# A decode step of two cached-attention layers: buffer base moved to a 256-byte boundary, and one long load per row and layer split unevenly over the DMA engines

## The chip, the core and the metric

The kernel runs on one core of one Trainium2 chip. A core has five engines that matter here: TensorE (PE in the profile; its weight loads are listed apart as PEld), VectorE (DVE), ScalarE (ACT), GpSimd (POOL) and SyncE (SP), which in this kernel issues every DMA. Transfers between the chip's main memory (HBM) and the on-chip buffer of 128 partitions (SBUF) are carried out by the core's 16 DMA engines. The metric is the device time of one execution in microseconds (us).

## The reference, cut to what matters

One token per sequence, eight sequences (B = 8), width D = 640, 32 heads of width 128, and a cache of 4096 keys and values per head. The block is applied twice, with the same caches and weights:

```python
def _A_ref(x, k_cache, v_cache, wq, wo):        # attention over the cache
    q = (x @ wq) as [B, 32, 1, 128]
    scores = einsum("bhqd,bhkd->bhqk", q, k_cache) * 128 ** -0.5
    o = einsum("bhqk,bhkd->bhqd", softmax(scores), v_cache)
    return o as [B, 1, 4096] @ wo
def _B_ref(x, w1, w2):                          # dense layer, 640 -> 1728 -> 640
    return relu(x @ w1) @ w2
x = A_x
x = x + _A_ref(layernorm(x), k_cache, v_cache, wq, wo)
x = x + _B_ref(layernorm(x), w1, w2)
x = x + _A_ref(layernorm(x), k_cache, v_cache, wq, wo)
x = x + _B_ref(layernorm(x), w1, w2)
```

Keys and values of one sequence are 32 x 4096 x 128 values each, 64 MiB for both in bfloat16. Both layers need them, so the two layers together read nearly 1 GB if little is kept between them; every byte is used for one multiplication per layer.

## The kernel before

The host lays keys (transposed) and values of a sequence side by side in one array `A_kv` of shape [8, 128, 131072]: for each sequence and each of the 128 partitions one contiguous row of 256 KiB, in the order in which the kernel reads it. The smallest piece that the kernel handles is a **unit**: 128 partitions x 2048 values (4 KiB per partition, 512 KB in all), a quarter of the keys or of the values of a pair of heads.

**The arena.** `arena` (L346) is one SBUF tile of G = 26 units. Loads put units of `A_kv` into it, PE uses each unit once per visit, and a unit's place is then free for another load. Keys are used at L575 (each 128 x 128 block is loaded as PE's weights, the query is the moving column), values at L563 (the softmax weights `P_sb` are PE's weights, the values move). For a sequence, the units that layer 0 read last stay in the arena (`keep`, 21 of them) for layer 1, and two more are parked in PSUM (`stash`), so that layer 1 begins with data that is already there.

**The order.** `plan` (L34) writes the whole program as one list of operations before anything is issued: pairs of heads (visits) of layer 0 of the next sequence alternate in blocks with those of layer 1 of the present one, and the tail of each layer (output projection, dense layer, norms) is put between matmuls as small steps. The list is executed in this order on every engine (a manual schedule: nothing is reordered). The planner keeps a rough clock of PE and of the loads; from the lead of the loads over PE it chooses how many units one load takes (`LEADS`, L22: 8, 4 or 2 units, otherwise 1), within `feed` (L109), which is called whenever a unit's place is freed and appends `("load", b, p, n, u)`: sequence, place in `A_kv`, number of units, place in the arena. A "long" load is one of 8 units: 128 rows of 32 KiB, 4 MB.

In the list there are 536 loads: 235 of one unit, 41 of two, 17 of three, 100 of four, 16 of five and 127 of eight. While the kept units hold most of the arena, around the change from layer 0 to layer 1 of each sequence, 27 to 29 loads of one unit follow each other; this happens eight times. Between these stretches of single units lie nine stretches with long loads, each with six to seventeen of them.

**The loads.** `do_load` (L527) issues one DMA on SP's queue for each load:

```python
def do_load(b, p, n, u):
    nc.sync.dma_start(out=arena[:, u * GW : (u + n) * GW], in_=A_kv[b, :, p * GW : (p + n) * GW])
```

Before it issues, SP waits until PE has finished with the units that are overwritten, and until the DMA eight before it has landed, since the completion semaphores are eight, taken in turn. PE in turn waits for the landing of a load before its first use of a unit of it.

**Where things lie.** Tiles lie in SBUF in the order of their pools: `consts` first, then the weights (`w1_sb`, `w2_sb`, `wq_sb`, `wo_sb`), then `arena`, then the small tiles (`sm`). The tile `wo_sum` (L339), 16 bytes per partition, is in `consts`; it holds row sums of `wo` that are computed once on DVE in `do_ws` (L407) and read by PE in `do_w` (L640). With it the weights and the arena start 32 bytes past a multiple of 256: the arena's first byte is at 119,072 of its partition.

Of the kernel before, what the change touches and what calls it, by code (L numbers as in the profile page):

```python
# [10 lines left out]
BF16 = mybir.dt.bfloat16  # L11
# [10 lines left out]
LEADS = ((9, 8), (6, 4), (5, 2))  # L22
SOON = 4
AHEAD = 2
BANK = 512
CAP = 20


# [5 lines left out]
def plan(B, NP, n_up, n_down):  # L34
# [35 lines left out]
    for which, i in slots:  # L70
        layer, b, hp = visits[i]
# [14 lines left out]
    lands = [0.0] * G  # L86
    where, kept, ready = {}, {}, {}
    ops, chains = [], []
    at = [0, 0]
    clock = [5.0, 6.0]  # L90

    def keeps(which, i, g):
# [7 lines left out]
    def place(x):  # L100

        return visits[x[1]][1], tile_at(NP, x[0], visits[x[1]][2]) * UNIT + x[2], keeps(*x)

    def room(n):

        us = [u for u in range(G - n + 1) if not any(owner[u : u + n])]
        return min(us, key=lambda u: max(freed[u : u + n])) if us else None

    def feed():  # L109

        while at[0] < len(stream):
            most = next((n for least, n in LEADS if clock[1] - clock[0] >= least), 1)
            most = min(most, max(1, (len(stream) - at[0]) // 2), max(1, (G - len(kept) - 2) // 3))
            b, p, keeping = place(stream[at[0]])
            n = 1
            while n < most and place(stream[at[0] + n]) == (b, p + n, keeping):
                n += 1
            u = room(n)
            if u is None:
                return  # L120
            for k, (which, i, g) in enumerate(stream[at[0] : at[0] + n]):
                ops.extend(("weights",) + w for w in weights.pop(i, []) if which == "K")
                owner[u + k] = True
                where[which, i, g] = u + k
                if keeping:
                    kept[which, b, visits[i][2], g] = u + k
            at[0] += n
            clock[1] = max(clock[1], clock[0] + 1.4) + 0.1 + 1.2 * n
            lands[u : u + n] = [clock[1] + 2] * n
            ops.append(("load", b, p, n, u))  # L130

    def find(which, i, g):
        u = where.get((which, i, g))
        return kept[which, visits[i][1], visits[i][2], g] if u is None else u

    def release(which, i, g):
        key = which, visits[i][1], visits[i][2], g
        u = where.pop((which, i, g), None)
        at[1] += 1
        if key in kept:  # L140
            if visits[i][0] == 0:
                return
            u = kept.pop(key)
        if visits[i][0] == 0 and stashed(which, i, g) is not None:
            ops.append(("stash", stashed(which, i, g), u))
        owner[u], freed[u] = False, at[1]
        x = uses[at[1] + SOON] if at[1] + SOON < len(uses) else None
        if x and visits[x[1]][0] and stashed(*x) is not None:
            u = where[x] = room(1)
            owner[u] = True  # L150
            lands[u] = clock[0] + 2
            ops.append(("unstash", stashed(*x), u))
        feed()
# [10 lines left out]
    def step():  # L164

        n = 0
        for c in sorted(chains, key=lambda c: c[0][0]):
            if not n or n + c[0][0] <= CAP:
                n += c[0][0]
# [13 lines left out]
    def finish(layer, b):  # L183
# [13 lines left out]
        return c  # L197

    feed()
    for which, i in slots:  # L200
        layer, b, hp = visits[i]
# [10 lines left out]
        for g in range(UNIT):  # L212
            u = find(which, i, g)
# [39 lines left out]
def kernel(  # L253
# [12 lines left out]
    nc = tc.nc  # L266
    P = nc.NUM_PARTITIONS
# [11 lines left out]
    GW = W // UNIT  # L279
# [10 lines left out]
    consts = ctx.enter_context(tc.tile_pool(name="consts", bufs=1))  # L290
    wres = ctx.enter_context(tc.tile_pool(name="wres", bufs=1))
    kv = ctx.enter_context(tc.tile_pool(name="kv", bufs=1))
    sm = ctx.enter_context(tc.tile_pool(name="sm", bufs=2))
# [13 lines left out]
    def load_weights(which, g=0):  # L307
# [15 lines left out]
        out=ident, in_=ident, pattern=[[-1, P]], compare_op=ALU.not_equal,  # L323
# [12 lines left out]
    for c in range(4):  # L336
        rows = slice(32 * c, 32 * c + CJ)
        nc.vector.tensor_copy(out=gsel[rows, :, c // 2], in_=ident[rows, rows])
    wo_sum = consts.tile([P, 2, 2, 2], BF16, name="wo_sum")  # L339
    eps_c = consts.tile([P, 1], FP32, name="eps_c")  # L340
    nc.vector.memset(eps_c, eps)
    xT = consts.tile([P, B, DC], FP32, name="xT")
# [1 line left out]
    q0 = consts.tile([P, H, B], BF16, name="q0")  # L344
    o1 = consts.tile([P, H, B], BF16, name="o1")
    arena = kv.tile([P, G * GW], BF16, name="arena")  # L346
    OR = 96 + CJ
    o_ps = ps.tile([P, CJ * Dh], FP32, name="o_ps")
    s_ps = ps.tile([P, 2, 2 * NJ], FP32, name="s_ps")
    blk_ps = ps.tile([P, BANK], FP32, name="blk_ps")  # L350
    oy_ps = ps.tile([P, BANK], FP32, name="oy_ps")
    stash_ps = [ps.tile([P, 2 * BANK], BF16, name=f"stash{n}_ps") for n in range(STASH * GW // (2 * BANK))]
    per = len(stash_ps) // STASH
    nc.vector.memset(o_ps, 0.0)

    up_parts = [range(f, min(f + 3, FC)) for f in range(0, FC, 3)]
    visits, ops = plan(B, NP, len(up_parts), DC)
    q1, s_tiles, P_tiles, m_tiles, o_tiles, blk, oy, invL, oT, nmax, st = ({} for _ in range(11))

# [154 lines left out]
    def do_stash(slot, u):  # L514
        for n, t in enumerate(stash_ps[slot * per : (slot + 1) * per]):
            nc.vector.tensor_scalar(
                out=t.bitcast(mybir.dt.int32),
                in0=arena[:, u * GW + n * 2 * BANK : u * GW + (n + 1) * 2 * BANK].bitcast(mybir.dt.int32),
                scalar1=0, scalar2=None, op0=ALU.bitwise_or,
            )  # L520

    def do_unstash(slot, u):
        for n, t in enumerate(stash_ps[slot * per : (slot + 1) * per]):
            copy = nc.vector.tensor_copy if n % 2 else nc.scalar.copy
            copy(out=arena[:, u * GW + n * 2 * BANK : u * GW + (n + 1) * 2 * BANK], in_=t)

    def do_load(b, p, n, u):  # L527
        nc.sync.dma_start(out=arena[:, u * GW : (u + n) * GW], in_=A_kv[b, :, p * GW : (p + n) * GW])

    def do_q0(g):  # L530

# [89 lines left out]
    def do_oc(i):  # L621
        o_tiles[i] = sm.tile([P, CJ, Dh], BF16, name="o_sb", bufs=1)
        nc.scalar.copy(out=o_tiles[i][:OR], in_=o_ps[:OR, :].rearrange("p (j d) -> p j d", j=CJ))  # L623

    def do_og(i):
        oy[i] = oy_ps[:, : 2 + DC * B]
        for j in range(CJ):
            nc.tensor.matmul(  # L628
                oy[i][:, :2], lhsT=o_tiles[i][:OR, j, :], rhs=gsel[:OR, j, :], start=(j == 0), stop=(j == CJ - 1)
            )  # L630
# [27 lines left out]
    def do_y(i):  # L658
# [3 lines left out]
        nc.vector.tensor_tensor(out=xT[:, b0 : b0 + nb, :], in0=xT[:, b0 : b0 + nb, :], in1=y, op=ALU.add)  # L662

    does = dict(WS=do_ws, S=do_s, YC=do_yc, load=do_load, stash=do_stash, unstash=do_unstash, weights=load_weights, mm=do_mm, M1=do_m1, T=do_t, M2=do_m2, B=do_b, E=do_e,
                L=do_l, I=do_i, OC=do_oc, OG=do_og, O=do_o, W=do_w, Y=do_y, C=do_finish, Q0=do_q0, Q=do_q, QC=take_q)

# [65 lines left out]
```

## Time and profile before

| | |
|---|---|
| median of 3 runs | 2388.94 us (2388.45 to 2391.3) |
| the profiled execution | 2390.05 us |
| its span, first to last instruction | 2388.2 us |
| granted TensorE clock | 1.0 |
| PE busy | 1281.9 us (54%) |
| PE weight loads busy | 792.0 us (33%) |
| DVE, ACT busy | 383.6 us (16%), 386.2 us (16%) |
| moved by DMA | 996.01 MB, mean 417 GB/s over the span |
| PE idle before L563, before L575 | 628.2 us, 313.7 us, nearly all ended by a load's landing |

Times and counts are of one profiled execution. Where the page gives a wait, it names the instruction that waited, what ended the wait, the total in us, how often, and the longest. A DMA of a tile is named by the tiles: `arena<-in_A_kv_dram` is a load of `do_load`. "SPq" is SP's queue of DMA issues. The chain that ended last is found by going back from the last instruction, at each step to what released it.

### The profile page before, as it was taken

To read this page: it belongs to the slowest core of one execution; us is meant where nothing else is said; L and a number is where in the kernel's file an instruction comes from. 1 tells how busy PE (TensorE), PEld (TensorE's weight loads), DVE (VectorE), ACT (ScalarE), POOL (GpSimd) and SP (SyncE) were. 2 spreads that over 40 slices of the span, in tenths; PEclk is the share of its full clock that TensorE was granted. 3 is DMA by queue.
4 is the path that set the end of the run, shared out by engine and by line. 5 is a ranking of instruction groups with operands and counts; after the bars stand their busy time and mean duration, and the time that the engine had idled before them with its cause. 6 is when DMAs were issued, how large, how long until landed. Compare 5 with 4: busy or idle time off the path is not lost.

```text
span 2388.2 us, 57845 instructions
## 1 busy us (share of the span) xinstructions
PE 1281.9 (54%) x26522; PEld 792.0 (33%) x26522; DVE 383.6 (16%) x1889; ACT 386.2 (16%) x1177; POOL 39.3 (2%) x190
## 2 busy tenths in 40 slices
PE   3437544574544844558444574446644466544845
PEld 2325322252323522225222352224422244222523
DVE  1103111121111211112111221112111121111211
ACT  1112111121111211112111121111211112111211
POOL 0000000000000000000000000000000000000000
DMA  9999999999999999999999999999999999999997
GB/s 409 426 426 392 429 427 430 426 385 430 429 429 424 397 428 427 433 420 398 431 427 430 405 412 428 427 431 403 416 428 428 427 398 414 427 430 426 392 429 308
DMA packets 78968, 996.01 MB, mean 417 GB/s; under 512 B 8836, under 2 KB 8836, under 8 KB 38916
## 3 DMA queue, kind: packets, MB, share of 16 engines
q1 hardware_dynamic: 78724, 992.32, 98.9%
q8 instruction: 207, 3.39, 0.6%
q14 instruction: 37, 0.30, 0.0%
HBM read 992.27 MB, written 0.01 MB: 415 GB/s over the span
## 4 chain that ended last, share of the span: by engine, by line
DMA 77%; PE 16%; ACT 3%; DVE 2%; issue 1%; POOL 0%; SPq 0%; POOLq 0%; DVEq 0%; ACTq 0%
DMA arena<-in_A_kv_dram 77%; PE s_ps L575 7%; PE o_ps L563 4%; ACT P_sb L604 2%; DVE hmx L589 1%; PE blk_ps L547 1%; PE oy_ps L628 1%; ACT nmax L600 1%; PE blk_ps L594 1%; PE oy_ps L450 1%; PE oy_ps L645 1%; PE blk_ps L585 1%; PE blk_ps L609 1%; DVE diag L591 0%; ACT o_sb L623 0%
## 5 line engine op out<-in xcount | busy, mean ns | idle before, releaser
L563 PE MATMUL o_ps<-arena,P_sb 128*4 128x512 bf16 x4096 | 559.4, 603 | 628.2 <-DMA arena<-in_A_kv_dram 625.9
L575 PEld LDWEIGHTS <-arena 128*128 128x128 bf16 x16384 | 495.2, 104 | 443.8 <-DMA arena<-in_A_kv_dram 418.2
L575 PE MATMUL s_ps<-q_97,arena 128*128 128x1 bf16 x8192 | 272.9, 166 | 313.7 <-DMA arena<-in_A_kv_dram 308.1
L563 PEld LDWEIGHTS <-P_sb 128*4 128x4 bf16 x4096 | 95.7, 82 | 710.7 <-issue 692.2
L600 ACT ACTIVATE nmax<-blk_ps 128x2 f32<-128x2 f32 x128 | 22.0, 172 | 1051.5 <-PE blk_ps L594 1051.5
L589 DVE TENSOR_REDUCE hmx<-blk_ps 2x1 f32<-2x128 f32 x256 | 71.3, 279 | 606.2 <-PE blk_ps L585 605.4
L623 ACT CAST o_sb<-o_ps 100x512 bf16<-100x512 f32 x256 | 149.8, 585 | 112.4 <-PE o_ps L563 109.5
L600 ACT ACTIVATE nmax<-blk_ps,q_scale 128x2 f32<-128x2 f32 x128 | 33.6, 262 | 652.7 <-PE blk_ps L594 650.5
L615 DVE TENSOR_REDUCE lsum<-blk_ps 128x2 f32<-128x64 f32 x256 | 57.4, 224 | 450.9 <-PE blk_ps L609 450.8
L581 DVE TENSOR_REDUCE mrow<-s_ps 128x2 bf16<-128x64 f32 x256 | 57.6, 225 | 334.7 <-PE s_ps L575 299.4
L609 PEld LDWEIGHTS <-onesb_c 128*128 128x128 bf16 x256 | 26.7, 104 | 200.7 <-issue 200.7
L604 ACT ACTIVATE P_sb<-s_ps,nmax,q_scale 128x32 bf16<-128x32 f32 x256 | 82.6, 373 | 4.3
L585 PE MATMUL blk_ps<-ident,mrow 128*2 128x128 bf16 x256 | 73.7, 288 | 0.0
L638 DVE TENSOR_TENSOR oT<-oy_ps,invL 128x2 bf16<-128x2 f32 x128 | 20.4, 159 | 320.6 <-PE oy_ps L628 320.6
L628 PE MATMUL oy_ps<-gsel,o_sb 100*128 100x2 bf16 x1024 | 66.1, 168 | 8.0 <-DVE xc L493 1.8
L594 PEld LDWEIGHTS <-onesb_c 2*128 2x128 bf16 x256 | 25.2, 98 | 125.2 <-issue 124.9
L609 PE MATMUL blk_ps<-P_sb,onesb_c 128*128 128x64 bf16 x256 | 57.2, 224 | 8.9 <-ACT P_sb L604 0.2
L604 ACT ACTIVATE P_sb<-s_ps,nmax 128x32 bf16<-128x32 f32 x256 | 59.4, 283 | 4.1
L628 PEld LDWEIGHTS <-o_sb 100*128 100x128 bf16 x1024 | 49.5, 108 | 23.5 <-ACT o_sb L623 10.0
L594 PE MATMUL blk_ps<-diag,onesb_c 2*128 2x2 bf16 x256 | 41.7, 163 | 25.8 <-DVE diag L591 0.4
L575 PE MATMUL s_ps<-q_30433,arena 128*128 128x1 bf16 x1024 | 34.5, 166 | 38.3 <-DMA arena<-in_A_kv_dram 37.4
L547 PE MATMUL blk_ps<-xq,wq_sb 128*128 128x1 bf16 x1280 | 52.2, 165 | 3.0 <-DVE hmx L589 2.6
(191 smaller groups left out, 822.3 us busy)
## 6 DMA issues: line engine op xcount, KB each, us to landing
arena<-in_A_kv_dram SPq DMA_DIRECT2D x127, 4096.0 KB, 25.1
arena<-in_A_kv_dram SPq DMA_DIRECT2D x100, 2048.0 KB, 24.3
arena<-in_A_kv_dram SPq DMA_DIRECT2D x235, 512.0 KB, 6.8
arena<-in_A_kv_dram SPq DMA_DIRECT2D x41, 1024.0 KB, 11.8
arena<-in_A_kv_dram SPq DMA_DIRECT2D x16, 2560.0 KB, 22.9
arena<-in_A_kv_dram SPq DMA_DIRECT2D x17, 1536.0 KB, 24.8
wq_sb<-in_A_wq_dram SPq DMA_DIRECT2D x4, 1280.0 KB, 30.2
wo_sb<-in_A_wo_dram SPq DMA_DIRECT2D x4, 1280.0 KB, 30.0
```

The lines of the kernel that those rows point to most:

```text
L547: nc.tensor.matmul(q_ps[:, h : h + 1], lhsT=wq_sb[:, g, c, (2 * n + h) * Dh : (2 * n + h + 1) * Dh], rhs=xlns[b][:, 0, c : c + 1], start=( ...
L563: nc.tensor.matmul(o_ps[32 * c : 32 * c + CJ, :], lhsT=P_tiles[i][:, h, j : j + CJ], rhs=arena[:, at + c * CJ * Dh : at + (c + 1) * CJ * D ...
L575: nc.tensor.matmul(s_tiles[i][:, j : j + 1], lhsT=arena[:, at + n * P : at + (n + 1) * P], rhs=q, start=True, stop=True)
L581: nc.vector.tensor_reduce(out=m_tiles[i], in_=s_tiles[i].rearrange("p (h j) -> p h j", h=2), axis=AX.X, op=ALU.max)
L585: nc.tensor.matmul(blk[i][:2, :P], lhsT=m_tiles.pop(i), rhs=ident, start=True, stop=True)
L589: nc.vector.tensor_reduce(out=hmx, in_=blk[i][:2, :P], axis=AX.X, op=ALU.max)
L594: nc.tensor.matmul(blk[i][:, P : P + 2], lhsT=ones_b, rhs=nmax.pop(i), start=True, stop=True)
L600: nc.scalar.activation(out=nm, in_=blk[i][:, P : P + 2], func=ACT.Copy, scale=less)
L604: nc.scalar.activation(out=P_tiles[i][:, h, :], in_=S[:, h, :], func=ACT.Exp, bias=nm[:, h : h + 1], scale=more)
L609: nc.tensor.matmul(blk[i][:, P + 2 :], lhsT=ones_p, rhs=P_tiles[i].rearrange("p h j -> p (h j)"), start=True, stop=True)
L623: nc.scalar.copy(out=o_tiles[i][:OR], in_=o_ps[:OR, :].rearrange("p (j d) -> p j d", j=CJ))
L628: nc.tensor.matmul(oy[i][:, :2], lhsT=o_tiles[i][:OR, j, :], rhs=gsel[:OR, j, :], start=(j == 0), stop=(j == CJ - 1))
```

## The change

Two edits.

The first moves the small tile `wo_sum` from the pool `consts` to the pool `sm`, which lies after the arena. All tiles between, the weights and the arena, move 32 bytes down: the arena starts at 119,040, a multiple of 256.

The second counts the loads of 8 units. The planner starts counting anew at each load of one unit, and marks a load of 8 units as "tilted" when it is the fifth since then. `do_load` issues a tilted load in three DMAs instead of one: partitions 0 to 111, then 112 to 119, then 120 to 127, with the same columns. Nine of the 127 long loads are marked, one in each of the nine stretches. The rest of the list of operations is the same.

```diff
@@ -23,6 +23,7 @@
 SOON = 4
 AHEAD = 2
 BANK = 512
+TILTED = (5,)
 CAP = 20
@@ plan
-    at = [0, 0]
+    at, long = [0, 0], [0]
@@ feed
             lands[u : u + n] = [clock[1] + 2] * n
-            ops.append(("load", b, p, n, u))
+            long[0] = 0 if n == 1 else long[0] + (n == LEADS[0][1])
+            ops.append(("load", b, p, n, u, n == LEADS[0][1] and long[0] in TILTED))
@@ the kernel's tiles
-    wo_sum = consts.tile([P, 2, 2, 2], BF16, name="wo_sum")
     eps_c = consts.tile([P, 1], FP32, name="eps_c")
...
     arena = kv.tile([P, G * GW], BF16, name="arena")
+    wo_sum = sm.tile([P, 2, 2, 2], BF16, name="wo_sum", bufs=1)
@@ do_load
-    def do_load(b, p, n, u):
-        nc.sync.dma_start(out=arena[:, u * GW : (u + n) * GW], in_=A_kv[b, :, p * GW : (p + n) * GW])
+    def do_load(b, p, n, u, tilted):
+
+        for rows in (slice(0, 112), slice(112, 120), slice(120, P)) if tilted else (slice(0, P),):
+            nc.sync.dma_start(out=arena[rows, u * GW : (u + n) * GW], in_=A_kv[b, rows, p * GW : (p + n) * GW])
```

## The prediction

> **What bounds the kernel now.** I read the slices first, then the chain, then two stretches set side by side.
>
> ```profile
> span 2388.2 us, 57845 instructions
> ...
> DMA  9999999999999999999999999999999999999997
> GB/s 409 426 426 392 429 427 430 426 385 430 429 429 424 397 428 427 433 420 398 431 427 430 405 412 428 427 431 403 416 428 428 427 398 414 427 430 426 392 429 308
> ...
> q1 hardware_dynamic: 78724, 992.32, 98.9%
> q8 instruction: 207, 3.39, 0.6%
> ...
> DMA 77%; PE 16%; ACT 3%; DVE 2%; issue 1%; POOL 0%; SPq 0%; POOLq 0%; DVEq 0%; ACTq 0%
> ```
>
> The DMA engines are busy in every slice, at 425 to 433 GB/s except in a dip about every five slices, and 77% of the chain that ended last is loads into `arena`. Beside the loads runs a small stream, q8: 207 instruction fetches. The dips are the stretches of single-unit loads, once per batch row:
>
> ```profile
> core 0: us, PE busy (x) PEld busy (x) DVE busy (x) ACT busy (x) POOL busy (x), PEclk, DMA share, GB/s
> 590.00:760.00 170.00, 79.47 (x1627) 47.41 (x1627) 22.76 (x115) 23.28 (x74) 0.00 (x0) 1.00 1.00 428
> 784.00:822.00 38.00, 32.73 (x724) 24.38 (x725) 9.49 (x51) 9.13 (x28) 4.82 (x23) 1.00 0.99 385
> ```
>
> In the long stretch PE is busy 47% of the time and the DMA engines set the pace; in the 38 us stretch PE is busy 86% and loads wait for it to free units. The chain of waits around the border of the two:
>
> ```profile
> 744.07 20.27 DMA arena<-in_A_kv_dram
> 764.41 21.03 DMA arena<-in_A_kv_dram
> 785.49 0.58 PE s_ps L575 x16
> ```
>
> So up to 785.49 us the chain is one load after another, and from there it is PE's. What ended the last DMA step is the completion of the load issued at 764.4. The trace's DMA records (start, duration and bytes of each packet, completion times; no engine's number) give that load's sixteen completions: 0, 0.5, 0.7, 1.1, 1.3, 1.5, 1.7, 1.8 us after the first, then 4.4, 4.8, 4.9, 5.0, 5.2, 5.3, 5.6, 5.8. The last of them is at 785.45 us, and PE starts there. **Eight engines run some 4 us behind the other eight, and PE waits for the slowest.** At the next dependent load the fast ones stand idle: first completions step by 4.3 us there, where a unit takes 1.28, while the last engine steps by 1.27 and never rests. The same jump ends each row's long stretch; the spread of completions just before it is 4.1, 5.9, 5.8, 5.5, 5.9, 5.8, 5.7 and 4.8 us, and 3.8 at the program's end.
>
> Why eight: packets on one engine follow each other within 3 to 4 ns, so they can be strung into sixteen chains. Each q8 fetch (16,384 bytes) breaks one chain for about 1.05 us and lengthens a packet beside it by about 0.5, and the chain that fetch n hits is the one that fetch n+8 hits (seen in three stretches of 160 to 180 us). So eight fixed engines carry all fetches, about three each per row.
>
> [...]the 40-row load of `x_bf` has ten completions. [...]the nearest case here is `w1`, whose odd rows begin 128 bytes off in HBM: some take 651 ns where the line through 16,384 bytes (614 ns) and 17,920 (671 ns) gives 647. [...]
>
> **The change, part by part.**
>
> 1. *Tilt.* The plan's list of operations stays as it is; nine of its 536 loads, each of 4 MB, become three DMAs. They are the fifth long load of each long stretch, so one comes before each of the eight borders and one before the end. A row of the load is 32,768 bytes and takes 1.216 us. Engines of the first half get nine rows instead of eight, those of the second seven: +1.216 and -1.216 us each time. If the eight that fetch are the second half, the last completion before each border comes 1.216 us sooner. It cannot be overtaken by the fast half: their latest stand at 1.1 to 2.7 us on the scale above, so after the tilt at 2.3 to 3.9, and the slow half's latest at 2.9 to 4.7. Only at the end is it close (1.4 + 1.2 against 3.8 - 1.2), and 1.20 is kept. From a border on the chain is PE's, so all that follows starts sooner by as much, and after each border the two groups are mixed again, so the gain is made anew: 8 x 1.216 + 1.20 = **10.9 us**.
> 2. *Its price.* Eighteen DMAs more on SP, about 0.45 us of SP each by the first issues (0.7, 1.2, 1.6, 2.1 us): 8 us in all. Behind them on SP stand the next loads. SP issues a long load 20 to 25 us before it lands, with a load or two still queued in front. Its longest wait, in us, times and the longest one, is for earlier loads:
>
> ```profile
> SPq L528 <- DMA arena<-in_A_kv_dram: 1139.9, 307, 13.5
> ```
>
> and the page's list of issues gives the time to landing:
>
> ```profile
> arena<-in_A_kv_dram SPq DMA_DIRECT2D x127, 4096.0 KB, 25.1
> ...
> arena<-in_A_kv_dram SPq DMA_DIRECT2D x235, 512.0 KB, 6.8
> ```
>
>    That cover hides it: 0. Without it, 0.9 us per tilt would be exposed. Completion semaphores go round eight lanes, so each tilt moves later DMAs two lanes on; a long stretch has three or four loads in flight, five or six with a tilt, so no lane is waited for. PE's first matmuls on the eight units wait for three lanes in place of one; PE idles half of that stretch: 0, at most 0.1 us times nine.
> 3. *Alignment.* `wo_sum` (16 bytes, in a 32-byte place) leaves the pool ahead of the weights, and `arena` moves from 119,072 bytes, 32 past a multiple of 256, to 119,040, a multiple. No instruction changes. No row with an aligned destination is in the trace, so I bound it: at least 0 (no packet or byte is added, which excludes a loss; writes may not care), at most the 3.7 ns per row of `w1`. I take 1.18 ns, the time of 32 bytes at the slope of the packet times. On the path lie the rows outside the single-unit stretches: (536 - 235 single loads + 10 weight loads) x 8 rows per engine = 2488, so 0 to 9.2 us, taken **2.9**. The other 1880 rows lie in stretches that PE sets: 0 taken, at most 7.
>
> Sum: 10.9 + 2.9 = 13.8 us. The profiled execution took 2390.05 us around its span of 2388.2, 1.1 above the median of 2388.94. So 2376.2 there and **2375.1** against the median.
>
> **Rivals.** A measurement of this kernel can tell about 0.2% (4.8 us) from no change.
>
> - *A, as summed:* 2375, from 2362 (alignment at its upper bounds, 16 us) to 2380 (alignment nothing, a little lost). For it: nine borders of one pattern, and a shift between the halves of 2.43 us per row, well inside the mean lag of 2.7 to 4.5.
> - *B, the fetches are not on the second half.* The profile shows a fixed set of eight, not which. If any of the late ones is among the first eight, the latest completion before each border comes later: 9 x 1.216 = +10.9, less 2.9, so 2397, slower by 0.33%; up to 2400 without the alignment's gain. It decides as soon as one engine with three fetches per row lies in the lower half. For it: nothing rules it out. Against it: [...]which half is a judgment, and I lean to the upper.
> - *C, the gain is given back.* After a border loads come in a loop of issue, landing and release of about five units. If the pieces of landing that PE waits for there are set by the backlog left on the slow engines and not by PE, the sooner start is waited away, and only the end's 1.2 and the alignment's 2.9 stay: 2385. Against it: PE is 86% busy there.
>
> **Numbers.** A 0.67, B 0.20, C 0.13. Faster by over 0.2%: A nearly whole and a third of C, 0.70; within: two thirds of C and the part of B where alignment pays most, 0.13; slower 0.17. The range runs from A's lower end to 2392, which takes in C and the lower part of B; most of B, under 0.2, is left out.
>
> **What would show it.** Right: completions before a border spread by about 3.4 us instead of 5.8; the fast group's idle step about 3 us instead of 4.3; the single-unit stretches unchanged in length but each starting some 1.5 us sooner per row than the last; 4 KB and 32 KB packets 1 ns shorter; SP's waits for loads unchanged but for a few us. Wrong: spreads of 7 to 8 us (B); spreads smaller but the borders at the old times (C); a packet time unchanged to the nanosecond (alignment nothing) or 3 ns shorter (its upper bound).

## The result, and the profile after

| | median, us | from to |
|---|---|---|
| before | 2388.69 (4 runs) | 2387.01 to 2391.3 |
| after | 2521.45 (4 runs) | 2519.42 to 2528.34 |

The ratio is 1.056, with an interval of 1.0538 to 1.0582. The forecast was 2375; the kernel became 133 us slower, far outside the range. From the page of the kernel after:

```profile
span 2519.4 us, 57892 instructions
...
DMA  9999999999999999999999999999999999999997
GB/s 410 334 432 400 433 310 432 430 382 405 370 433 427 392 426 339 434 409 405 329 431 432 400 416 363 389 431 385 428 332 432 428 387 431 357 402 426 387 421 204
...
q1 hardware_dynamic: 78868, 992.32, 98.6%
q8 instruction: 207, 3.39, 0.5%
...
DMA 78%; PE 16%; ACT 3%; DVE 2%; issue 1%; SPq 0%; POOL 0%; POOLq 0%; DVEq 0%; ACTq 0%
```

The bytes are the same and the shares of the chain are nearly the same; the DMA row still shows full tenths in every slice. Only the rate tells: beside the dips of the single-unit stretches (380 to 405) there are new ones, down to 310 and 204. "Busy" in that row means that a packet is under way, not that bytes move at full rate: a window below has a share of 0.99 at 157 GB/s. There are nine new dips, as many as marked loads. The trace's list of DMA issues shows them by size:

```profile
arena<-in_A_kv_dram SPq DMA_DIRECT2D x118, 4096.0 KB, 26.3
...
arena<-in_A_kv_dram SPq DMA_DIRECT2D x235, 512.0 KB, 6.9
...
arena<-in_A_kv_dram SPq DMA_DIRECT2D x9, 3584.0 KB, 38.9
...
arena<-in_A_kv_dram SPq DMA_DIRECT2D x18, 256.0 KB
```

The 112-row part is an eighth smaller than a whole load and takes 38.9 us from issue to landing where a whole one takes 26.3. One of the nine, on the chain of waits in order of time (start, length, what):

```profile
289.31 24.61 DMA arena<-in_A_kv_dram
...
318.85 0.33 SPq L532
319.23 0.33 SPq L532
319.61 42.95 DMA arena<-in_A_kv_dram
...
367.32 23.99 DMA arena<-in_A_kv_dram
```

SP's issues on the chain cost 0.33 us each; the step of 43 us, between ordinary ones of 24 to 25, is the transfer itself. The same place in four windows (columns as in the prediction's windows: busy us and instructions of PE, PEld, DVE, ACT and POOL, granted clock, share of DMA time, GB/s):

```profile
300.00:320.00 20.00, 8.74 (x190) 5.42 (x186) 2.42 (x12) 3.31 (x10) 0.00 (x0) 1.00 1.02 440
320.00:340.00 20.00, 9.33 (x194) 5.51 (x193) 2.22 (x12) 3.31 (x10) 0.00 (x0) 1.00 1.03 339
340.00:360.00 20.00, 0.00 (x0) 0.00 (x0) 0.20 (x1) 0.00 (x0) 0.00 (x0) 1.00 0.99 157
360.00:380.00 20.00, 11.22 (x193) 5.87 (x193) 3.24 (x16) 4.49 (x12) 0.00 (x0) 1.00 0.97 413
```

The third of these windows in the kernel before:

```profile
340.00:360.00 20.00, 11.21 (x193) 5.72 (x192) 2.90 (x15) 3.82 (x12) 0.00 (x0) 1.00 1.01 428
```

For 20 us PE does nothing at all, the DMA share is 0.99, and 157 GB/s arrive. In the four windows the kernel before moves 426, 427, 428 and 430. The four rates fall short by 362 together; 362 x 20 us / 428 = **16.9 us lost at this one load**. Nine such are 152 us; the arena's new place gives some 20 back, as e1 below shows.

The DMA records of the load say how. The completions of the load ahead of it (four units, undivided) come at 330.4 to 337.6 us, the sixteen of the 112-row part at 346.7 to 360.2, the eight of each 8-row part at 351.0 to 360.0 and 356.8 to 362.6. So the marked load and the whole long one behind it (366.1 to 371.9) take some 34 to 36 us after the one ahead, where two whole long loads take 16 rows x 1.213 = 19.4. And packets of 32,768 bytes, a row each, are no longer alike: the median is 1213 ns, but 1658 of them take over 1300 ns (129 before), half of these over 2280, the longest 5879. That is more than the 1152 rows of the nine loads: rows of the loads ahead and behind are held up too. What the packets take above their usual time comes to 131 us per engine (3.8 before), most of the loss.

### The profile page after: what moved, and what is told of

Read it like the earlier page. It is cut to its first block, busy times and chain, and to the rows that moved or that the text cites. A ratio compares the mean times of both kernels' runs of the same rounds, so it can differ in the third digit from the quotient of the medians.

```text
span 2519.4 us, 57892 instructions
## 1 busy us (share of the span) xinstructions
PE 1278.8 (51%) x26522; PEld 788.9 (31%) x26522; DVE 383.6 (15%) x1889; ACT 387.0 (15%) x1177; POOL 39.6 (2%) x190
## 2 busy tenths in 40 slices
DMA packets 79112, 996.01 MB, mean 395 GB/s; under 512 B 8980, under 2 KB 8980, under 8 KB 39060
## 4 chain that ended last, share of the span: by engine, by line
DMA 78%; PE 16%; ACT 3%; DVE 2%; issue 1%; SPq 0%; POOL 0%; POOLq 0%; DVEq 0%; ACTq 0%
DMA arena<-in_A_kv_dram 78%; PE s_ps L579 7%; PE o_ps L567 4%; ACT P_sb L608 2%; DVE hmx L593 1%; PE blk_ps L551 1%; PE oy_ps L632 1%; ACT nmax L604 1%; PE blk_ps L598 1%; PE blk_ps L589 1%; PE blk_ps L613 0%; PE oy_ps L649 0%; DVE diag L595 0%; PE oy_ps L452 0%; ACT o_sb L627 0%
## 5 line engine op out<-in xcount | busy, mean ns | idle before, releaser
L642 DVE TENSOR_TENSOR oT<-oy_ps,invL 128x2 bf16<-128x2 f32 x128 | 20.3, 159 | 319.5 <-PE oy_ps L632 319.5
## 6 DMA issues: line engine op xcount, KB each, us to landing
arena<-in_A_kv_dram SPq DMA_DIRECT2D x118, 4096.0 KB, 26.3
arena<-in_A_kv_dram SPq DMA_DIRECT2D x9, 3584.0 KB, 38.9
```

## The experiments

**Theory P, the places.** A row of a whole load takes 1.213 us, 27.0 GB/s, steadily; with the parts under way it takes up to 5.9. P says that this comes from the places in SBUF that are written at one moment: the rows of a part lie otherwise than those that a whole load writes together, the engines that write them hold each other up, and rows that follow on those engines wait. Which engine writes which rows, no trace shows. The figures that the expectations give for P are the author's estimates; what they were counted from was not shown, and the comparisons between runs below do without it.

**Rivals.** That the unequal shares cost (nine rows against seven); that more and smaller DMAs cost as such; that the read side (rows of HBM) is what collides; and for the rest, that the loss is in the new place of the arena and not in the parts.

The first four experiments tried the two edits apart and two other ways of cutting the nine loads. Each ratio is to the kernel before as it ran beside the experiment (2387.3 to 2388.7 us).

### e1, aligned: the move without the parts

```diff
-TILTED = (5,)
+TILTED = ()
```

> The changed kernel with no load marked, so that only the 32-byte move of the weights and the arena is left. In the trace of the changed kernel the packets outside the split loads take 1213, 611 and 309 ns where they took 1216 to 1224, 614 to 621 and 313 to 320. If that is the alignment, some 5 ns on each of the 2488 rows per engine outside the single-unit stretches: 12 us less than before, 2374 to 2378. If the alignment is without effect and the shorter packets come from the split loads in some way: 2388 as before, packets of 1216 ns again.

Measured: 2368.21 us (2364.98 to 2370.99), ratio 0.9917 (0.9902 to 0.9932). From its page:

```profile
span 2366.6 us, 57845 instructions
...
GB/s 409 428 429 396 432 429 434 427 396 433 430 432 427 406 429 430 433 425 404 428 432 431 415 418 430 430 433 410 423 430 430 429 410 421 431 432 428 396 431 314
```

The new dips are gone, and most slices lie 1 to 5 GB/s above before. So the move is a gain, by some 20 us and not the 2.9 of the prediction or the 12 expected here, and the parts cost 2521.45 - 2368.21 = 153 us, 17.0 for each of the nine.

### e2, tilt only: the parts without the move

```diff
+    wo_sum = consts.tile([P, 2, 2, 2], BF16, name="wo_sum")
     eps_c = consts.tile([P, 1], FP32, name="eps_c")
...
-    wo_sum = sm.tile([P, 2, 2, 2], BF16, name="wo_sum", bufs=1)
```

> The kernel before with the nine split loads alone; the arena stays 32 bytes past the boundary. If the two parts add up and the split is the whole loss: the time of the changed kernel plus what the alignment gives, 2521 + 12 = 2533 (2528 to 2540), some 16 us for each of the nine. If the loss came from the move of the tiles or needs both parts: near 2389.

Measured: 2546.38 us, ratio 1.0653 (1.0629 to 1.0677). The two edits add up to within a few us: the move is worth 25 us with the parts and about 20 without. That is 13 us above what was expected; its four runs spread over 18 us, and it is not explained further.

### e3 and e4: eight parts of 16 rows, in blocks and in combs

```diff
-        for rows in (slice(0, 112), slice(112, 120), slice(120, P)) if tilted else (slice(0, P),):
+        for rows in [slice(16 * k, 16 * k + 16) for k in range(8)] if tilted else (slice(0, P),):
```

and for e4 `slice(k, P, 8)` in place of the block. The kernel after has 144 packets under 512 B more than the one before (8980 and 8836), as many as its nine loads have completions more, 9 x (16 + 8 + 8 - 16). e3 and e4 both have 9844, 1008 = 9 x 7 x 16 more than e1: each of the eight parts has sixteen completions, one row for each of the 16 engines. So the shares are equal, and the number and size of DMAs are the same in both. The rows of a block lie side by side, those of a comb eight partitions apart.

> Aligned; the nine marked loads are split evenly, into eight DMAs of 16 consecutive partitions, one row for each of the 16 engines in each DMA, so no engine gets more than another. Theory P [...]: [...] about 2638. Theory S (it is the splitting itself, more DMAs, more completions, more waits): as the next kernel, a few us each, 2380 to 2420. Theory T (the uneven shares alone): as the aligned kernel, 2376.

> The same nine loads in eight DMAs of 16 rows again, one row for each engine, but every eighth partition (k, k+8, ..., k+120). Bytes, DMAs and rows per engine are those of the kernel with 16 consecutive partitions; only which partitions go together differs[...]. Theory P: [...]about 2463. Theories S and T: the same time as with consecutive partitions.

Measured: e3 2551.21 us, ratio 1.0688 (1.0656 to 1.0721); e4 2488.49, ratio 1.0425 (1.0406 to 1.0445). So nine loads in equal shares lose more than the tilt does (e3), and the same number of DMAs of the same size loses 63 us less when its rows lie further apart. Neither unequal shares nor the number of DMAs explains that difference. The order is the one of P's estimates, but the size isn't (they had 2638 and 2463): e3 took 87 us less than that and e4 25 more. Blocks cost 20.3 us per load over e1, combs 13.4.

The DMA records show the steps. In e4 the completions of one part follow those of the part ahead mostly at 2.4 to 2.6 us, twice a row's 1.213. The rows of a comb lie at least eight partitions apart, so it isn't only neighbours that hinder each other. In e3 the parts step by some 3.25 us on average, 2.7 times a row's time. The engines stand 3 to 10 us apart when such a load begins, so those of one moment can be at different parts; what this does to the two costs is not shown. No run spreads sixteen rows in a third way, so whether some spread would cost nothing is not shown either.

### e5 and e6: which side collides

The read side and the write side of the eight parts are taken apart. e5 reads blocks and writes combs:

```diff
+        whole = slice(0, P)
+        for to, fro in [(slice(k, P, 8), slice(16 * k, 16 * k + 16)) for k in range(8)] if tilted else [(whole, whole)]:
+            nc.sync.dma_start(out=arena[to, u * GW : (u + n) * GW], in_=A_kv[b, fro, p * GW : (p + n) * GW])
```

and e6 has `to` and `fro` exchanged: it reads combs and writes blocks.

> As the two kernels with eight DMAs of 16 rows, but each DMA reads 16 consecutive rows of HBM and writes every eighth partition (so the units of the nine loads hold their rows in another order, and the output differs). Theory P [...]: as with combs on both sides, 2488 us (2475 to 2500). Theory H (what is shared is on the HBM side, by which rows are read together): as with consecutive rows on both sides, 2551.

> The other way round: each DMA reads every eighth row of HBM and writes 16 consecutive partitions (the output differs for the same reason). Theory P: as with consecutive partitions on both sides, 2551 us (2535 to 2565). Theory H: as with combs on both sides, 2488.

Measured: e5 2489.56 us, ratio 1.0425 (1.0404 to 1.0445), against e4's 2488.49; e6 2558.03, ratio 1.0705 (1.0687 to 1.0722), against e3's 2551.21. The rows that are read make no difference beyond a few us; the rows that are written decide. The windows around one marked load, with the columns as above, first the two that write combs, e4:

```profile
600.00:620.00 20.00, 5.19 (x111) 3.23 (x112) 1.43 (x7) 1.66 (x5) 0.00 (x0) 1.00 1.02 330
620.00:640.00 20.00, 5.01 (x106) 2.96 (x98) 1.21 (x6) 1.66 (x5) 0.00 (x0) 1.00 0.99 229
640.00:660.00 20.00, 10.16 (x204) 5.95 (x203) 2.85 (x14) 3.46 (x11) 0.00 (x0) 1.00 1.00 428
660.00:680.00 20.00, 11.06 (x231) 6.69 (x224) 2.98 (x15) 4.34 (x12) 0.00 (x0) 1.00 0.99 424
```

and e5:

```profile
600.00:620.00 20.00, 6.63 (x115) 3.31 (x114) 1.64 (x8) 2.28 (x8) 0.00 (x0) 1.00 1.05 335
620.00:640.00 20.00, 4.78 (x101) 2.84 (x97) 1.21 (x6) 1.77 (x7) 0.00 (x0) 1.00 0.96 238
640.00:660.00 20.00, 9.46 (x198) 5.82 (x195) 2.42 (x12) 3.44 (x11) 0.00 (x0) 1.00 1.02 437
660.00:680.00 20.00, 10.97 (x243) 7.30 (x244) 3.20 (x16) 3.59 (x10) 0.00 (x0) 1.00 0.98 420
```

then the two that write blocks, e3:

```profile
600.00:620.00 20.00, 9.32 (x194) 5.76 (x194) 2.42 (x12) 3.31 (x10) 0.00 (x0) 1.00 1.01 431
620.00:640.00 20.00, 9.32 (x194) 5.67 (x193) 2.42 (x12) 3.31 (x10) 0.00 (x0) 1.00 1.06 270
640.00:660.00 20.00, 0.00 (x0) 0.00 (x0) 0.00 (x0) 0.00 (x0) 0.00 (x0) 1.00 0.95 169
660.00:680.00 20.00, 9.32 (x194) 5.78 (x195) 2.42 (x12) 3.31 (x10) 0.00 (x0) 1.00 1.00 431
```

and e6:

```profile
600.00:620.00 20.00, 7.58 (x179) 5.03 (x176) 1.86 (x9) 1.81 (x6) 0.00 (x0) 1.00 1.02 438
620.00:640.00 20.00, 8.33 (x189) 5.53 (x186) 2.16 (x12) 3.31 (x10) 0.00 (x0) 1.00 1.04 377
640.00:660.00 20.00, 4.65 (x97) 2.79 (x96) 1.21 (x6) 1.65 (x5) 0.00 (x0) 1.00 1.01 164
660.00:680.00 20.00, 6.24 (x111) 3.35 (x115) 1.64 (x8) 1.92 (x6) 0.00 (x0) 1.00 0.95 320
```

The loads arrive at somewhat different times in the four, so the sum of the four rates is what compares. In e1 it is 433 + 424 + 439 + 428 = 1724; in e4 1411 and in e5 1430, which is 14.5 and 13.6 us of transfer missing at 431 GB/s; in e3 1301 and in e6 1299, 19.6 and 19.7 us. The median times give 13.4 and 20.3 per load for e4 and e3: the loss is where the marked loads are, and its size goes with the partitions that are written.

### e7 and e8: the two kinds of part in the change

e7 cuts the loads into 112 and 16 rows, with sixteen completions each (8980 packets under 512 B, 9 x 16 more than e1): seven rows and one for each engine, so that all shares are equal. e8 issues the 112 rows alone and leaves the other 16 out.

```diff
-        for rows in (slice(0, 112), slice(112, 120), slice(120, P)) if tilted else (slice(0, P),):
+        for rows in (slice(0, 112), slice(112, P)) if tilted else (slice(0, P),):
```

and for e8 `(slice(0, 112),)`.

> Aligned; the nine marked loads in two DMAs, 112 rows and 16 rows, so that each engine gets 7 + 1 rows: no engine gets more. Theory P[...] some 60% of the 153 us between the changed kernel and the aligned one: 2440 to 2480. Theory T (the uneven shares): none of it, 2368. If the two parts of 8 rows do all the harm and the 112 rows none: below 2420.

> Aligned; of the nine marked loads only partitions 0 to 111 are loaded, the other 16 rows are left out (the output differs). By bytes alone 1.2 us less for each load, 2357. Theory P [...] 2385; if it is above 2420, the 112 rows alone cost more than that count gives.

Measured: e7 2498.66 us, ratio 1.0462 (1.0445 to 1.0479), above the 2440 to 2480 estimated; e8 2447.35, ratio 1.0243 (1.0228 to 1.0258), far above the 2385 estimated and the 2357 of the bytes alone. Over e1, per load:

| nine loads as | lost per load, us |
|---|---|
| 112 rows alone (e8) | 8.8 |
| 112 + 16 (e7) | 14.5 |
| 112 + 8 + 8 (after) | 17.0 |
| eight combs (e4) | 13.4 |
| eight blocks (e3) | 20.3 |

e8 has no DMA more than e1 and moves fewer bytes (991.30 MB, 996.01 in e1), and it loses 79 us: a load needn't be cut into more DMAs to lose. With equal shares e7 still loses 130 us. The other 23 of the change's 153 go with the two 8-row parts in place of one of 16, and so with the uneven shares. The 112 rows cost most: they move a row less per engine, 1.2 us, and end 8.8 us later, so 10.0 us. The 16 rows that follow cost 14.5 - 8.8 = 5.7 us where a row takes 1.2. That the written side decides was shown for blocks and combs; for the 112 rows it was not tried, and why they cost 10.0 us is not shown.

What the uneven shares do can be seen at the eight borders of the prediction, where PE waits for the slowest engine. There a load's sixteen completions spread by 4.8 to 7.8 us in the kernel after, 7.2 on average, and by 3.9 to 5.8 in e1, 5.1 on average. In e3, e4 and e7, where the shares are equal, the average is 5.4 to 5.6, though these kernels lose 120 to 183 us; in e2, with the same uneven shares, it is 7.4. So the wider spread comes with the uneven shares and not with the slow rows. At 2.1 us more at each of eight borders that is at most 17 us, most of the 23.

### e9, tags: which engines fetch

The loads are whole and the arena is aligned. After the second and the fifth long load of each stretch one more DMA reads 8 rows of 512 bytes into a small tile:

```diff
+    tag = sm.tile([8, 256], BF16, name="tag", bufs=1)
...
+        nc.sync.dma_start(out=arena[:, u * GW : (u + n) * GW], in_=A_kv[b, :, p * GW : (p + n) * GW])
+        if tilted:
+            nc.sync.dma_start(out=tag, in_=A_kv[b, 0:8, p * GW : p * GW + 256])
```

> The aligned kernel with whole loads; behind the second and the fifth long load of each stretch SP issues one more DMA of 8 rows of 512 bytes into a small tile that nobody reads. [...] its packets have a size of their own, so in the DMA records they tell which of the sixteen chains belong to the first eight. The prediction's case A: the chains that the fetches of q8 hit are those without a tag. Case B: some or all of those that are hit have a tag. Time as the aligned kernel, 2365 to 2372.

Measured, in one run: 2369.55 us, as e1. The eighteen DMAs leave 144 packets of 512 bytes; the trace has eight chains of packets with such a packet and eight without, so the DMAs of 8 rows fell on the same eight engines. These are the first half of the prediction, which gets nine rows of a marked load, 7 + 1 + 1, where the others get seven; how the engines are numbered the trace doesn't show. The fetches go round eight engines as read before the change. Of the eight places in the round, six break a chain without a tag and two, next to each other, break a chain with one; at those two the gap is 860 to 875 ns, at the others mostly 903 to 960.

### e10: how far off the boundary matters

The aligned kernel with a tile of 64, 128 or 256 bytes ahead of the arena:

```diff
+    pad = consts.tile([P, 32], BF16, name="pad")
+    nc.vector.memset(pad[:, 0:1], 0.0)
     arena = kv.tile([P, G * GW], BF16, name="arena")
```

> The aligned kernel with 64 bytes put ahead of the arena, which then starts 64 bytes past a multiple of 256; the weights keep their places. Theory M (any start off a multiple of 256 costs every row of the loads about the same): the time before, 2389, packets of 1216 to 1224 ns. Theory N (the price is that of a start that is no multiple of 64): as aligned, 2368. If the gain came from the weights' places and not the arena's: 2368 too, with packets of 1213.

> The same with 128 bytes[...]. Theory M: 2389. Theory N: 2368.[...]

> The same with 256 bytes: the arena at a multiple of 512. Theory M, with 256 as the whole of it: as aligned, 2368. If a multiple of 512 brings the same again: 2350.

| arena's start past a multiple of 256 | median, us | ratio to before | packet of 4,096 / 32,768 bytes, mean ns of those near the usual time |
|---|---|---|---|
| 32 (before) | 2388.7 | | 161.1 / 1217.7 |
| 64 | 2384.38 | 0.9987 (0.998 to 0.9994) | 161.0 / 1216.8 |
| 128 | 2382.33 | 0.9977 (0.9968 to 0.9986) | 160.5 / 1216.6 |
| 0 (e1) | 2368.21 | 0.9917 (0.9902 to 0.9932) | 159.1 / 1213.0 |
| 0, a multiple of 512 (pad of 256) | 2366.28 | 0.9911 (0.9896 to 0.9926) | 159.1 / 1213.0 |

Against the pad of 256, which ran beside them, 64 and 128 bytes off cost 18 and 16 us, and 32 bytes, the kernel before at 2387.65 in these runs, 21: most of the cost comes with any of the three. A multiple of 512 brings nothing more that can be told. The pad of 256 leaves the order of tiles as in the others, so the gain lies in the addresses and not in the pad.

The expectation has the weights keep their places. They don't: the pad stands in `consts`, ahead of the weights, and moves them by as many bytes as the arena. So the times alone don't tell the arena's place from that of the weights; the packets do, since almost all of them are the arena's. Taken over all sizes, packets are longer than in e1 by 15.4, 12.9 and 11.3 us per engine at 32, 64 and 128 bytes off. The instruction fetches change as well: a fetch takes 1060 to 1064 ns on average in the three kernels off the boundary, and 934 in e1 and with the pad of 256. At 26 fetches for each fetching engine that is 3.3 us (an estimate). Together that makes 18.7, 16.2 and 14.6 of the 21, 18 and 16 us. Why a fetch is shorter when the arena lies on the boundary is not shown.

## Why the prediction was wrong, point by point

**The bound: right.** Loads set the pace, and PE waits for the slowest engine of each. All of what follows comes through that: of the 153 us between e1 and the kernel after, 148.2 lie in the long stretches and the end, 4.6 in the single-unit ones.

**Step 1, the tilt: failed at "a row of the load is 32,768 bytes and takes 1.216 us".** That time was read from whole loads and was applied to rows cut in another way. With the parts under way a row takes up to 5.9 us. So a marked load did not end 1.216 us later on one half of the engines and sooner on the other: it cost 17 us more. The prediction counted how many rows an engine takes, but did not ask where in SBUF the rows of one moment lie. No whole load in the trace of before could have shown it; a part is an operation that this trace doesn't contain, and its price should have been left open upward.

**The premise "the eight that fetch are the second half": false as well.** e9 shows six of the second half and two of the first. That is the condition from which rival B decides, so by the prediction's own reasoning the latest completion before a border would not have come sooner as summed, even without the loss in the parts. B's mark, spreads of 7 to 8 us, came at six of the eight borders (7.5 to 7.8 us; 4.8 and 6.8 at the others), and as e3, e4 and e7 show, it comes with the uneven shares. So B's mechanism ran too, but its sum was 10.9 us, and the kernel is 124 us beyond its 2397: it is the small part of the loss. Case A had 0.67 on a judgment that nothing in the trace of before bore out.

**Step 2, the price of eighteen DMAs on SP: right.** SP's issues cost 0.33 us each, and e9, with eighteen DMAs more and no part of a load, runs as e1. SP's waits did grow, though "unchanged but for a few us" was expected:

```profile
SPq L532 <- DMA arena<-in_A_kv_dram: 1272.2, 315, 21.6
```

132 us more than before, as much as the span grew: SP waits for loads that land late, and is not why they do.

**Step 3, alignment: right in sign, too small.** The rows of 32 KiB are 4.7 ns shorter, where 1.18 was taken and 3.7 was the upper bound; the bound came from `w1`, whose rows are off on the read side, and the arena's rows, off on the written side, cost more. The shorter fetches were in no term. The other rows "lie in stretches that PE sets: 0 taken". Counted from the landing of the last long load to that of the last single unit, these stretches fell from 312.0 to 303.9 us between the kernel before and e1, and the rest by 13.5, together 21.6, against 2.9. But the stretches are 303.9 us with the arena 64 and 128 bytes off as well, where packets of a unit are within 0.6 ns of those before, and 298.1 with the pad of 256, each in one execution. So how much of these 8.1 us is the alignment's is not shown.

**Rival C** could not be seen: no border came sooner by the tilt.

## What to carry to other kernels

Keep a load in one DMA of all 128 partitions wherever it can be; to shift work between engines by cutting off rows is dear: nine loads of 536 cut into complete sets of parts cost 5 to 8% over the same kernel without the cuts (e4 5.1, e6 8.0), and in e3 to e6 the cost went with the rows of SBUF that are written together. When a time is taken from a trace, ask in what the new operation will differ from the traced one, here in the rows that are written together. Start large tiles that DMA fills at a multiple of 256 bytes: it cost nothing and gave 0.8 to 0.9%, and e1 and the pad of 256, at 2368 and 2366 us, beat both kernels of this case.

## What the runs showed of the hardware that was not expected

- **The written rows decide.** The same rows read, but written elsewhere, moved the time by 62 us (e5 against e3) and 70 (e6 against e4). A nearly full DMA share at less than half the rate is what this looks like in a profile (0.95 at 169 GB/s in e3, 0.99 at 157 in the kernel after): the engines are busy, with packets of two to five times their usual time (in the kernel after half of the 1658 long ones took 2.3 to 5.9 us, 1.213 is usual).
- **A split with equal shares also costs**, and the most harmless kind that was tried, every eighth row, still lost 13.4 us on a load whose eight rows per engine take 9.7.
- **Writes off a 256-byte boundary cost 1.4 to 2.0 ns per row of 4 KiB and 3.6 to 4.7 ns per row of 32 KiB**, least at 128 bytes off, and an instruction fetch in such a kernel takes 0.13 us longer. The reason isn't shown by these runs.
- **Instruction fetches fall on eight fixed engines, six of one half and two of the other**, and stop each for mostly 0.86 to 0.96 us at a time in the aligned kernel (e9).
